# Block-sparse attention and a Hyena mixer in one kernel: mask copies in an earlier slot, stores in a later one, another order before the main loop

## The chip, the cores and the metric

The kernel runs on one core of a Trainium2 chip. The metric is the time of one execution in microseconds (us) on the device. The kernel before takes 345.78 us (median of 3 runs, 345.19 to 347.83).

## The reference

Two parts, one after the other. The first is block-sparse attention: 4 batches x 8 heads, 768 positions, head size 64. Keys are averaged over blocks of 64 positions; each query takes the three blocks with the highest causal gate score, and its own block. The second part, a Hyena mixer, projects the attention's result (768 x 512 for each batch) to three parts, convolves the second with a filter over the sequence by Fourier transforms, multiplies the three and projects once more.

```python
gate_scores = np.einsum('bhsd,bhnd->bhsn', q, k_rep)          # k_rep: block means of k
gate_scores = np.where(causal, gate_scores, -1000000000.0)
top_idx = np.argsort(gate_scores, axis=-1)[..., -top_k:]      # top_k = 3, and the own block
scores = scale * np.matmul(q, k.transpose(0, 1, 3, 2))        # masked to those blocks, causal
attn = softmax(scores);  x = attn @ v
x1, x2, x3 = split(x @ w_proj)
x2_conv = irfft(rfft(x2) * rfft(filter_fft))
out = (x1 * x2_conv * x3) @ w_out
```

## The kernel before

**Slots.** The 32 heads (4 batches x 8) are worked one after the other, each in three slots (`s` = 0, 1, 2). The order of all instructions is written out by hand: the loop at the end of the kernel goes over the slots, and what it emits first stands first on each engine. A slot computes one of three groups of score matmuls (`scores`, L393), their exponential on ACT (L396) and the causal cut of the diagonal blocks on POOL (`diagonals`, L404). One slot later follow the product with the values (`product`, L415), the inverse of the sums on ACT (L422, L423) and, another slot later, the normalisation on DVE (L433).

**Preparing a head.** The sync engine's queue (SP) issues the loads of keys, queries and values some heads ahead (L106, L110, L114), 192 KB each. For head n+4, in slots 0 and 1 of head n: DVE casts the query to fp16 and takes the remainder (`split_query`, L302, L304), POOL casts the key (`cast_key`, L295) and scales the remainder (`low_query`, L307), and SP issues a DMA transpose of both to the tile qkT (`turn_query`, L312). That instruction waits on SP until POOL has written; what stands behind it on SP waits too.

**The mask.** The block choice goes into the scores as 12 additional rows of qkT (rows 64 to 75 of the query's half), which meet one-hot rows on the key's side. For two heads at once, n+2 and n+3 at an even head n: `gate` (slot 1) computes the gate scores on TensorE (L331) and picks the blocks on DVE (L334 to L344); `turn_mask` (slot 2) is a DMA transpose on SP to the tile gmT (L350); `place_mask` copies 12 rows of gmT into each of the two qkT by DMA (L366), in slot 1 of the odd head n+1, behind that slot's `turn_query`. The first scores of an even head need its copy. Heads 0 and 1 have another way, `turn_first_mask`: six transposes on TensorE (L358) and a copy on ACT (L360).

**Units of the mixer.** `plan` puts one unit of the mixer into most slots from head 9 on, for the batch whose attention is done; the last batch's units run after the last head. `unit_out` (L533) computes 128 rows of the result, ACT copies them to the tile osb (L536), and the store (L539) is issued on SP one slot later.

**Setup.** Before the first slot the kernel prepares heads 0 to 3 and the first part of the Fourier tables: products of positions on TensorE, brought into one turn by DVE, POOL and DVE (`phase_round` L199, `phase_turns` L205, `sines` L214 and L215). `small_constants` (POOL) writes the causal bias and own-block tables that `gate` uses. The dictionary `setup` puts further work into slots: the filter's rows are loaded in heads 2 to 4, folded in heads 4 to 6 (`filter_rows`, L588 to L591), and turned into a spectrum in slot 2 of heads 6, 7 and 8 (`filter_spectrum`): after six matmuls each of two or three results is made by one scaled copy on ACT from PSUM (L605) and one combined multiply-add on DVE (L606).

Of the kernel before, what the change touches and what calls it, by code (L numbers as in the profile page):

```python
# [9 lines left out]
FP32 = mybir.dt.float32  # L10
# [7 lines left out]
def kernel(  # L18
# [39 lines left out]
    xtp = ctx.enter_context(tc.tile_pool(name="xtp", bufs=2))  # L58
    p2 = ctx.enter_context(tc.tile_pool(name="p2", bufs=1))
    p2b = ctx.enter_context(tc.tile_pool(name="p2b", bufs=2))  # L60
    outp = ctx.enter_context(tc.tile_pool(name="outp", bufs=3))


    ps_big = ctx.enter_context(tc.tile_pool(name="ps_big", bufs=2, space=bass.MemoryType.PSUM))
# [43 lines left out]
    def load_query(n):  # L108
        queries[n] = hpool.tile([P, SC, D], FP32, name="q_nat", tag="q_nat")
        nc.sync.dma_start(queries[n], q_r[divmod(n, H)])  # L110
# [43 lines left out]
    def key_mask(i):  # L154
        nc.gpsimd.tensor_scalar(qk16s[i][:, 1, :, D:D + NBLK], in0=eblk, scalar1=MASK, scalar2=0.0,
                                op0=ALU.mult, op1=ALU.add)
# [10 lines left out]

    lsc = const.tile([P, 1], FP32)

    def small_constants():  # L170
        nc.gpsimd.memset(cbias, 0.0)
        nc.gpsimd.affine_select(
            out=cbias[0:64], in_=cbias[0:64], compare_op=ALU.is_ge,
            fill=-CBIG, base=0, pattern=[[2, SC], [0, 2], [-1, NBLK]], channel_multiplier=0)
        nc.gpsimd.affine_select(
            out=cbias[64:128], in_=cbias[64:128], compare_op=ALU.is_ge,
            fill=-CBIG, base=1, pattern=[[2, SC], [0, 2], [-1, NBLK]], channel_multiplier=0)
        for h in range(2):
            nc.gpsimd.tensor_scalar(ownm[:, :, h, :], in0=eblk, scalar1=1.0, scalar2=-1.0,
                                    op0=ALU.mult, op1=ALU.add)  # L180

    FC = const.tile([P, HC, F], fp)
    FS = const.tile([P, HC, F], fp)
# [22 lines left out]
                                scalar2=-float(S2), op0=ALU.add, op1=ALU.mult)  # L206


    sign16 = const.tile([P, 1], fp)
    sign = const.tile([P, 1], FP32)  # L210

    def sines(i):
        pr, ka = phases.pop(i)
        nc.vector.tensor_add(pr, pr, ka[:, 0:F])  # L214
        nc.scalar.activation(FS[:, i, :], pr, AF.Sin, bias=0.0, scale=TWO_PI / S2)  # L215
        if i == HC - 1:
            nc.vector.tensor_scalar(sign16, in0=pr[:, 0:1], scalar1=4.0 / S2, scalar2=None,
                                    op0=ALU.mult)
            nc.vector.tensor_copy(sign, sign16)

    def cosines(i):

# [67 lines left out]
                                       in1=kr[:, 0:w, 0, :], op0=ALU.mult, op1=ALU.subtract)  # L290
        sums[g] = kr

    def cast_key(n):
        g, i = group_of[n]
        nc.gpsimd.tensor_copy(qk16s[n % NB][:, 1, :, 0:D], keys[g][:, i])  # L295

    rems = {}

# [230 lines left out]
    def unit_out(st, scn):  # L529
        yT = st["yT"]  # L530
        op = one_tile("op")
        for cc in range(DC):
            nc.tensor.matmul(op, lhsT=yT[:, cc, P * scn:P * (scn + 1)], rhs=wo[:, cc, :],  # L533
                             start=(cc == 0), stop=(cc == DC - 1))
        osb = outp.tile([P, Dm], FP32, name="osb", tag="osb")
        nc.scalar.copy(osb, op)  # L536

        def later():
            nc.sync.dma_start(out[st["b"], P * scn:P * (scn + 1), :], osb)  # L539
        return later  # L540

    X2, X13, F1, F2, O = unit_x2, unit_x13, unit_f1, unit_f2, unit_out

# [49 lines left out]
    def filter_spectrum(j):  # L593
        sl = slice(P * j, P * (j + 1))
        hc, hs_ = pair("hsp", Dm)
        for i in range(HC):
            nc.tensor.matmul(hc, lhsT=FC[:, i, sl], rhs=fil[:, 0, i, :],
                             start=(i == 0), stop=(i == HC - 1))
        for i in range(HC):
            nc.tensor.matmul(hs_, lhsT=FS[:, i, sl], rhs=fil[:, 1, i, :],  # L600
                             start=(i == 0), stop=(i == HC - 1))

        def put(dst, first, s0, second, s1, op):
            t = p2b.tile([P, Dm], FP32, name="turn", tag="t1")
            nc.scalar.mul(t, second, s1)  # L605
            nc.vector.scalar_tensor_tensor(out=dst, in0=first, scalar=s0, in1=t,  # L606
                                           op0=ALU.mult, op1=op)
        cosB = tw0[:, 0:1] if j == 0 else tw[:, 0, j:j + 1]
        put(Asb[:, j, :], hc, tw[:, 0, j:j + 1], hs_, tw[:, 1, j:j + 1], ALU.add)
        put(Bsb[:, j, :], hs_, cosB, hc, tw[:, 1, j:j + 1], ALU.subtract)  # L610
        if j == 0:
            put(A2, hc, tw0[:, 0:1], hs_, tw0[:, 1:2], ALU.add)

    def weights(dst, src, cols, ns):
        nc.gpsimd.dma_start(out=dst[:, ns, cols],
# [4 lines left out]
    def at(n, slot, fn, *args):  # L620
        setup.setdefault((n, slot), []).append((fn, args))

    at(0, 0, key_sums_mm, 2, range(SC))
    at(0, 0, key_sums_copy, 2)
    at(0, 1, key_sums_turn, 2)
    at(0, 1, key_sums_split, 2)
    at(0, 2, gate, [2, 3])
    at(0, 2, turn_mask, [2, 3])
    at(2, 1, turn_weights)
    at(2, 2, make_flip)  # L630
    for i in range(HC):
# [14 lines left out]
    nc.vector.memset(lsc, 1.0)  # L646
    nc.vector.memset(lsc[64:128, :], 1.0 / LO)
    nc.vector.memset(qk16s[0][:, 1, :, D + NBLK:P], 0.0)
    for i in range(HC):
        phase_mm(i)  # L650
    phase_round(0)
# [1 line left out]
    phase_round(1)  # L653
    sines(0)
    phase_turns(1)
    key_mask(0)
    split_query(0)
    cast_key(0)
    low_query(0)
    turn_query(0)  # L660
    key_sums_mm(0, range(SC))
    sines(1)
    key_sums_copy(0)
    key_sums_mm(1, range(SC))
    key_sums_turn(0)
    nc.vector.memset(qk16s[1][:, 1, :, D + NBLK:P], 0.0)
    key_mask(1)
    cast_key(1)
    small_constants()
    split_query(1)  # L670
    low_query(1)
    turn_query(1)
    load_query(3)
    load_key(3)
    load_value(0)
    key_sums_split(0)
    key_sums_copy(1)
    key_sums_turn(1)
    phase_round(2)
    key_sums_split(1)  # L680
    for gm16 in gm16s:
        nc.gpsimd.memset(gm16, 0.0)
    phase_turns(2)
    sines(2)
    id_f16 = const.tile([P, P], fp)
    nc.gpsimd.memset(id_f16, 0.0)
    nc.gpsimd.affine_select(
# [11 lines left out]
    cast_key(2)  # L699
    low_query(2)  # L700
    turn_query(2)
    load_value(1)
    gate([1])
    turn_first_mask(1)
    nc.gpsimd.memset(v16s[0][:, :, D:P], 1.0)
    cast_value(0)
    split_query(3)
    cast_key(3)
    low_query(3)
    turn_query(3)  # L710
    for i in range(1, NB):
        nc.gpsimd.memset(v16s[i][:, :, D:P], 1.0)
    load_key(4)
    load_key(5)
    load_query(4)
    key_loads = {0: [6], 1: [7], 2: [8], 3: [9, 10], 4: [11]}


    xTs, stages, later = {}, {}, []
    for slot in range(max(units) + 1):  # L720
        n, s = divmod(slot, 3)
        todo, later = later, []
        if n < NH:
            if n % H == 0 and s == 0:
                xTs[n // H] = xtp.tile([P, DC, S], fp, name="xT", tag="xT")
            scores(n, s)
            if s == 2:
                scores_left[0] -= 1
        for fn in todo:
            fn()  # L730
        if n < NH:
            diagonals(n, s)
            if s == 0:
                for m in key_loads.get(n, [n + 7]):
                    if m < NH:
                        load_key(m)
                if n + 5 < NH:
                    load_query(n + 5)
                if n + 2 < NH:
                    load_value(n + 2)  # L740
                if n + 2 in group_at and n:
                    key_sums_turn(group_at[n + 2])
                if n + 4 < NH:
                    split_query(n + 4)
                    cast_key(n + 4)
                    low_query(n + 4)
                if n + 2 in group_at and n:
                    key_sums_split(group_at[n + 2])
            elif s == 1:
                if n + 4 < NH:  # L750
                    turn_query(n + 4)
                if n % 2 == 0 and 0 < n < NH - 2:
                    gate([n + 2, n + 3])
                elif n % 2 == 1 and n + 1 < NH:
                    place_mask(n + 1)
                    place_mask(n + 2)
            else:
                if n % 2 == 0 and 0 < n < NH - 2:
                    turn_mask([n + 2, n + 3])
                if n + 1 < NH:  # L760
                    cast_value(n + 1)

            if n + 3 in group_at and n:
                key_sums_mm(group_at[n + 3], (2 * s, 2 * s + 1))
                if s == 2:
                    key_sums_copy(group_at[n + 3])
        for fn, args in setup.get((n, s), []):
            fn(*args)
        for b, fn, *args in units.get(slot, []):
            if b not in stages:  # L770
                stages[b] = new_stage(b, xTs[b])
            act = fn(stages[b], *args)
            if act is not None:
                later.append(act)

        pn, ps = divmod(slot - 1, 3)
        if 0 <= pn < NH:
            product(pn, ps)
            if ps != 1:
                half = min(ps, 1)  # L780
                inverse_sum(pn, half)
                later.insert(0, lambda pn=pn, half=half: normalise(pn, half, xTs[pn // H]))
    for fn in later:
        fn()


# [28 lines left out]
```

## Time and profile before

The profiled execution took 347.45 us; its span, from the first to the last of the program's instructions, is 345.7 us.

| | |
|---|---|
| median of 3 runs | 345.78 us |
| profiled execution, its span | 347.45 us, 345.7 us |
| busy: TensorE (PE) | 268.8 us, 78% |
| busy: weight loads (PEld) | 138.3 us, 40% |
| busy: VectorE (DVE) | 206.4 us, 60% |
| busy: ScalarE (ACT) | 204.4 us, 59% |
| busy: GpSimd (POOL) | 186.1 us, 54% |
| transfers of SP's queue | 43.43 MB, 62.2% of 16 DMA engines |
| transfers of POOL's queue | 2.10 MB, 6.0% |
| mean granted TensorE clock | 0.904 |
| first scores of heads 0, 2, 12, 24 | 18.8, 41.3, 139.6, 242.2 us |

"Busy" is time in which an engine executed. A wait has a releaser, which the profile infers from semaphores: "PE sps L393 <- DMA qkT<-gmT" is idle time of TensorE before the score matmuls that ended when a mask copy landed. SPq is the queue that SP issues DMAs from; its instructions are issues, and the transfers run later on 16 shared DMA engines. POOL's queue casts and loads the weights. The granted clock is the share of full speed that the throttle leaves TensorE.

### The profile page before, as it was taken

To read this page: it belongs to the slowest core of one execution; us is meant where nothing else is said; L and a number is where in the kernel's file an instruction comes from. 1 tells how busy PE (TensorE), PEld (TensorE's weight loads), DVE (VectorE), ACT (ScalarE), POOL (GpSimd) and SP (SyncE) were. 2 spreads that over 40 slices of the span, in tenths; PEclk is the share of its full clock that TensorE was granted. 3 is DMA by queue.
4 is the path that set the end of the run, shared out by engine and by line. 5 is a ranking of instruction groups with operands and counts; after the bars stand their busy time and mean duration, and the time that the engine had idled before them with its cause. 6 is when DMAs were issued, how large, how long until landed. Compare 5 with 4: busy or idle time off the path is not lost.

```text
span 345.7 us, 5124 instructions
## 1 busy us (share of the span) xinstructions
PE 268.8 (78%) x1555; PEld 138.3 (40%) x1555; DVE 206.4 (60%) x568; ACT 204.4 (59%) x326; POOL 186.1 (54%) x336
## 2 busy tenths in 40 slices
PE   4267493967497695889679988995999879989785
PEld 3133241433142252445334544453445446535442
DVE  5616462634456099377945788688357965546750
ACT  2334492755766164557757777676677669953234
POOL 7633261865455229387753375868233847622670
PEclk9996876787769699899969999999699999999999
DMA  8796979998569889768778686667866511021004
GB/s 160 136 192 106 175 168 215 180 189 151 95 105 178 150 121 152 127 108 151 149 163 208 137 194 147 137 100 158 177 151 152 120 53 27 2 93 61 32 0 182
DMA packets 150379, 45.85 MB, mean 133 GB/s; under 512 B 145128, under 2 KB 146512, under 8 KB 150352
## 3 DMA queue, kind: packets, MB, share of 16 engines
q1 hardware_dynamic: 144976, 43.43, 62.2%
q0 software_dynamic: 5376, 2.10, 6.0%
q8 instruction: 12, 0.20, 0.2%
q14 instruction: 15, 0.12, 0.1%
HBM read 24.64 MB, written 6.29 MB: 89 GB/s over the span
## 4 chain that ended last, share of the span: by engine, by line
PE 42%; POOL 14%; ACT 13%; DVE 11%; DMA 10%; issue 7%; SPq 4%; DVEq 0%; ACTq 0%; POOLq 0%
DMA qkT<-gmT 8%; PE sps L393 7%; PE oT L415 6%; PE op L533 5%; ACT ex L396 4%; PE krp L263 4%; SPq L312 3%; ACT den L422 3%; PE x2a L461 3%; PE x2b L461 2%; POOL ex L404 2%; PE x13b L500 2%; PE x13a L500 2%; ACT den L423 2%; POOL PQ L489 1%
## 5 line engine op out<-in xcount | busy, mean ns | idle before, releaser
L396 ACT ACTIVATE ex<-sps 128x1024 f16<-128x1024 f32 (+2 forms) x96 | 88.0, 917 | 59.4 <-PE sps L393 57.4
L404 POOL TENSOR_SCALAR_AFFINE_SELECT ex<-ex 128x128 f16<-128x128 f16 (+1 forms) x128 | 47.3, 380 | 104.2 <-ACT ex L396 103.7
L393 PE MATMUL sps<-qkT 76*128 76x384 f16 (+2 forms) x288 | 62.2, 332 | 33.8 <-DMA qkT<-gmT 33.8
L415 PE MATMUL oT<-ex,v 128*128 128x384 f16 (+2 forms) x288 | 59.7, 314 | 11.6 <-POOL ex L404 6.5
L433 DVE TENSOR_TENSOR xT<-oT,den 64x384 f16<-64x384 f32 x64 | 35.2, 550 | 47.4 <-ACT den L423 45.7
L393 PEld LDWEIGHTS <-qkT 76*128 76x128 f16 x288 | 27.7, 109 | 49.5 <-DMA qkT<-gmT 30.4
L415 PEld LDWEIGHTS <-v 128*128 128x128 f16 x288 | 27.8, 103 | 44.7 <-issue 27.5
L422 ACT ACTIVATE den<-oT 64x384 f32<-64x384 f32 x64 | 31.1, 485 | 22.1 <-PE oT L415 20.9
L500 PEld LDWEIGHTS <-wp 128*128 128x128 f16 x256 | 24.8, 99 | 24.8 <-issue 10.0
L423 ACT ACTIVATE den<-den 64x384 f32<-64x384 f32 x64 | 33.3, 520 | 2.0
L263 PE MATMUL krp<-k_nat,eblk 128*12 128x256 f32 (+2 forms) x132 | 28.3, 356 | 1.9 <-POOL dft_ka L205 1.6
L533 PE MATMUL op<-wo,yT 128*128 128x512 f16 x96 | 27.2, 416 | 2.0 <-POOL yT L525 1.8
L500 PE MATMUL x13b<-xT,wp 128*128 128x384 f16 x116 | 24.1, 331 | 5.9 <-ACT x1sb L504 4.0
L489 POOL TENSOR_TENSOR PQ<-t,t 128x512 f16<-128x512 f32 x12 | 15.2, 1271 | 23.1 <-DVE t L482 22.9
L500 PE MATMUL x13a<-xT,wp 128*128 128x384 f16 x116 | 24.3, 332 | 0.0
L302 DVE CAST qk<-q_nat 128x384 f16<-128x384 f32 x32 | 17.9, 559 | 10.4 <-DMA q_nat<-in_q_dram 10.2
L505 DVE TENSOR_TENSOR gx<-x1sb,x13b 128x384 f32<-128x384 f16 x29 | 16.0, 551 | 12.5 <-PE x13b L500 8.3
L304 DVE TENSOR_TENSOR rem<-q_nat,qk 128x384 f32<-128x384 f32 x32 | 21.2, 664 | 2.5
L536 ACT COPY osb<-op 128x512 f32<-128x512 f32 x24 | 14.0, 585 | 13.6 <-PE op L533 12.6
L307 POOL TENSOR_SCALAR qk<-rem 128x384 f16<-128x384 f32 x32 | 16.3, 510 | 9.3 <-DVE rem L304 6.9
L525 POOL TENSOR_TENSOR yT<-gx,yy 128x384 f16<-128x384 f32 x16 | 16.0, 999 | 6.6 <-DVE yy L521 6.2
L317 POOL CAST v<-v_nat 128x384 f16<-128x384 f32 x32 | 19.0, 593 | 0.0
(129 smaller groups left out, 406.8 us busy)
## 6 DMA issues: line engine op xcount, KB each, us to landing
q_nat<-in_q_dram SPq DMA_DIRECT2D x32, 192.0 KB
k_nat<-in_k_dram SPq DMA_DIRECT2D x32, 192.0 KB
v_nat<-in_v_dram SPq DMA_DIRECT2D x32, 192.0 KB
out_dram<-osb SPq DMA_DIRECT2D x24, 256.0 KB
wp<-in_moe_w_proj_dram POOLq DMA_DIRECT2D x12, 128.0 KB, 5.2
fa<-in_moe_filter_fft_dram SPq DMA_DIRECT2D x3, 256.0 KB
fb<-in_moe_filter_fft_dram SPq DMA_DIRECT2D x3, 256.0 KB
qkT<-gmT SPq DMA_DIRECT2D x30, 18.0 KB
```

Source lines behind the costliest of these rows:

```text
L263: nc.tensor.matmul(sums[g][0:NBLK, 0:w * D], lhsT=eblk[:, c, :], rhs=keys[g][:, 0:w, c, :], start=(c == 0), stop=(c == SC - 1))
L304: nc.vector.tensor_sub(rems[n], q_nat, qk16[:, 0, :, 0:D])
L317: nc.gpsimd.tensor_copy(vals[n][:, :, 0:D], values.pop(n))
L393: nc.tensor.matmul(sps[:, col:col + qe - qs], lhsT=turned[n][0:76, 1, kc, :], rhs=qT[0:76, qs:qe], start=True, stop=True, skip_group_check ...
L396: nc.scalar.activation(ex[:, lo:hi], sps[:, lo:hi], AF.Exp, bias=0.0, scale=scale)
L404: nc.gpsimd.affine_select(out=sub, in_=sub, compare_op=ALU.is_ge, fill=0.0, base=0, pattern=[[0, cnt], [1, P]], channel_multiplier=-1)
L415: nc.tensor.matmul(oT[:, qs - HALF * half:qe - HALF * half], lhsT=vals[n][:, kc, :], rhs=exps[n, src][:, col:col + qe - qs], start=first, ...
L422: nc.scalar.activation(den[64:128, :], oT[64:128, :], AF.Ln, bias=0.0, scale=1.0)
L423: nc.scalar.activation(den[64:128, :], den[64:128, :], AF.Exp, bias=0.0, scale=-1.0)
L433: nc.vector.tensor_tensor(out=dst, in0=oT[0:64, :], in1=den[64:128, :], op=ALU.mult)
L500: nc.tensor.matmul(dst, lhsT=wp[:, dc2, base:base + P], rhs=xT[:, dc2, hs:hs + HALF], start=(dc2 == 0), stop=(dc2 == DC - 1))
L533: nc.tensor.matmul(op, lhsT=yT[:, cc, P * scn:P * (scn + 1)], rhs=wo[:, cc, :], start=(cc == 0), stop=(cc == DC - 1))
```

## The change

- `place_mask` for heads n+1 and n+2 moves from slot 1 of the odd head n, behind `turn_query`, to its slot 0, behind the loads and ahead of the next `turn_query`. It begins with heads 4 and 5: heads 2 and 3 now take the way of heads 0 and 1 (one `gate` each, six transposes on TensorE, a copy on ACT), in slot 2 of head 0 and slot 1 of head 1.
- A store is issued two slots after its unit (one after the last head), from a list, and osb has four buffers in place of three.
- Before the first slot: queries, keys and values of heads 0, 1, 3 and 4 are loaded in another order, some before the transposes of queries 1 and 2; the keys of heads 0 and 1 are cast on ACT in place of POOL; the gate's buffers are cleared on DVE in place of POOL; the last phase step comes earlier; `small_constants` is split in two. The gate and mask of head 1 and the preparation of query 3 move into slot 0 of head 0, query 4 into slot 1.
- `filter_spectrum` copies both results from PSUM on ACT once; the scaled copies are then made by DVE from those copies.
- The sign for the cosine table is computed from the sine table in slot 2 of head 0.

```diff
-    def small_constants():
+    def small_constants(half):
...
+    def time_sign():
+        nc.vector.tensor_scalar(sign, in0=FS[:, 0, 0:1], scalar1=0.0, scalar2=2.0,
+                                op0=ALU.is_gt, op1=ALU.mult)
+        nc.vector.tensor_scalar(sign, in0=sign, scalar1=-1.0, scalar2=None, op0=ALU.add)
...
-        def later():
-            nc.sync.dma_start(out[st["b"], P * scn:P * (scn + 1), :], osb)
-        return later
+        stores.append((slot, out[st["b"], P * scn:P * (scn + 1), :], osb))
...
+        hcs = p2b.tile([P, Dm], FP32, name="hcs", tag="t1")
+        hss = p2b.tile([P, Dm], FP32, name="hss", tag="t2")
+        nc.scalar.copy(hcs, hc)
+        nc.scalar.copy(hss, hs_)
         def put(dst, first, s0, second, s1, op):
-            t = p2b.tile([P, Dm], FP32, name="turn", tag="t1")
-            nc.scalar.mul(t, second, s1)
+            t = p2b.tile([P, Dm], FP32, name="turn", tag="t2")
+            nc.vector.tensor_scalar(t, in0=second, scalar1=s1, scalar2=None, op0=ALU.mult)
             nc.vector.scalar_tensor_tensor(out=dst, in0=first, scalar=s0, in1=t,
                                            op0=ALU.mult, op1=op)
...
     split_query(0)
-    cast_key(0)
+    cast_key(0, nc.scalar.copy)
+    small_constants(0)
     low_query(0)
     turn_query(0)
+    load_query(3)
+    load_key(3)
+    load_value(0)
...
     turn_query(1)
-    load_query(3)
-    load_key(3)
-    load_value(0)
+    load_value(1)
+    load_key(4)
+    load_query(4)
+    phase_round(2)
+    phase_turns(2)
...
     for gm16 in gm16s:
-        nc.gpsimd.memset(gm16, 0.0)
-    phase_turns(2)
-    sines(2)
+        nc.vector.memset(gm16, 0.0)
...
+    def prepare(n, s):
+        if s == 0:
...
+            if n % 2 == 1 and 1 < n < NH - 2:
+                place_mask(n + 1)
+                place_mask(n + 2)
...
+        elif s == 1:
+            if n + 4 < NH:
+                turn_query(n + 4)
+            if n == 1:
+                gate([3])
+                turn_first_mask(3)
+            elif n % 2 == 0 and n < NH - 2:
+                gate([n + 2, n + 3])
...
+    def prepare_first(s):
+        if s == 0:
+            gate([1])
+            turn_first_mask(1)
+            key_sums_mm(2, range(SC))
+            ready_query(3)
+            turn_query(3)
+            load_key(6)
+            load_query(5)
+            load_value(2)
+            for i in range(1, NB):
+                nc.gpsimd.memset(v16s[i][:, :, D:P], 1.0)
+        elif s == 1:
+            key_sums_copy(2)
+            key_sums_turn(2)
+            key_sums_split(2)
+            ready_query(4)
+            turn_query(4)
+        else:
+            gate([2])
+            turn_first_mask(2)
+            cast_value(1)
...
+        while stores and stores[0][0] <= slot - (2 if n < NH else 1):
+            _, dst, osb = stores.pop(0)
+            nc.sync.dma_start(dst, osb)
```

## The prediction

> **What bounds the kernel now.** I read the page's groups first: the score matmuls (L393) are TensorE's largest group, and all of their idle time has one releaser. Columns after the bars: busy us and mean ns, then idle us before and what ended it.
>
> ```profile
> L393 PE MATMUL sps<-qkT 76*128 76x384 f16 (+2 forms) x288 | 62.2, 332 | 33.8 <-DMA qkT<-gmT 33.8
> ```
>
> The table of waits (total us, times, longest) gives the size of one; the chain of waits of the DMA-issuing queue shows what that queue itself stands behind.
>
> ```profile
> PE sps L393 <- DMA qkT<-gmT: 33.8, 10, 6.0
> ```
>
> ```profile
> SPq L539 <- ACT osb L536: 71.0, 24, 17.5
> SPq L312 <- POOL ex L404: 32.9, 10, 6.9
> ```
>
> So TensorE stands still 33.8 us, ten times, always at the first scores of an even head, until that head's mask rows have been copied by DMA. The queue's own timeline says why they come late (start us, issue us):
>
> ```profile
> 47.22 1.24 SPq L350 DMA_TRANSPOSE gmT<-gm  x1
> 48.51 0.58 SPq L581 DMA_DIRECT2D fa<-in_moe_filter_fft_dram  x1
> 49.13 0.43 SPq L582 DMA_DIRECT2D fb<-in_moe_filter_fft_dram  x1
> 49.61 1.02 SPq L106 DMA_DIRECT2D k_nat<-in_k_dram  x2
> 50.67 0.54 SPq L110 DMA_DIRECT2D q_nat<-in_q_dram  x1
> 51.26 1.15 SPq L114 DMA_DIRECT2D v_nat<-in_v_dram  x1
> 52.52 2.89 SPq L312 DMA_TRANSPOSE qkT<-qk  x1
> 55.46 1.52 SPq L366 DMA_DIRECT2D qkT<-gmT  x2
> ```
>
> The masks (L366) go out behind the query transpose (L312), which waits for POOL and needs 2.89 us to issue; the scores of head 4 start at 57.61, after 6.01 us of idling. Last, stretches of the trace: busy time of the engines, granted clock, DMA share, GB/s.
>
> ```profile
> 42.00:44.50 2.50, 2.50 (x21) 1.40 (x20) 0.49 (x2) 2.03 (x3) 1.01 (x3) 0.50 1.11 234
> 44.50:46.50 2.00, 2.00 (x10) 1.18 (x9) 1.89 (x13) 1.92 (x3) 1.01 (x3) 0.50 0.02 2
> 52.00:56.00 4.00, 0.00 (x0) 0.00 (x0) 1.37 (x5) 0.40 (x1) 0.75 (x2) 0.75 1.26 224
> 41.30:139.60 98.30, 69.94 (x355) 33.28 (x356) 52.65 (x155) 56.23 (x85) 52.19 (x95) 0.80 0.93 155
> ```
>
> Heads 2 to 11 (41.3 to 139.6) have no full engine: TensorE 70 of 98 us. The DMA share reads 0.93, but single stretches read 1.26 and others 0.02, so 0.93 is about three quarters of what the engines reach here.
>
> **The masks, heads 4 to 12.** The copies now go out right after the loads of the odd head's first slot, ahead of the query transpose of the second. Two cases. Where transfers are queued up, the copy saves the bytes of the transpose ahead of it: 393 KB at the 234 GB/s above is 1.7 us. That holds at heads 4 (idle 6.01) and 6 (idle 2.93): 2 x 1.7 = 3.4. Where the queue stood waiting for POOL, the copies leave much earlier: head 8, at 83.1 (last load issued) instead of 91.28, so all of its 3.19; head 10, 108.6 instead of 112.48, with 1.7 us of bytes less ahead: landing about 111 where TensorE was free at 110.44, so 4.8 of 5.37; head 12, 130.9 instead of 133.76 and landing near 135, so all 4.6. Together **16.0 us**. What the copies newly wait for on this queue is the landing of the mask transpose itself, issued two to three loads before; at head 4 it was out 5 us before that point.
>
> **The masks, heads 16 to 28.** Idle 2.68, 0.62, 3.23, 0.53. Here something else is late next: at 24 the projection (L533) needs yT, which POOL finishes at 240.63 (start 239.63, 1.00), while it started at 243.01, so 2.4; at 16 POOL ends at 174.19 against 175.94, so 1.7; the small ones whole. **5.2 us.**
>
> **The clock behind the stalls.** TensorE rows right after a stall:
>
> ```profile
> 242.18 1.03 PE L393 MATMUL sps<-qkT 76*128 76x128 f16 x4 [3.23 <-DMA qkT<-gmT]
> 243.01 1.91 PE L533 MATMUL op<-wo,yT 128*128 128x512 f16 x4
> ```
>
> The same groups elsewhere take 0.60 (233.34) and 0.97 (185.08). Over the first five groups after 242.18 (1.03, 1.91, 0.85, 0.95, 1.87) against their undisturbed rows (0.60, 0.97, 0.49, 0.55, 0.97) that is 3.0 us. TensorE is the bound there, so I count 5 us for heads 16 and 24 together, and nothing in heads 2 to 11, where slower matmuls have slack (bounds 0 and 5 x 1.7 = 8 more).
> The Trainium skill (TensorE: Matmul & The Clock Gate, What's actually happening) says that an idle window of about 3.4 us halves the clock until about 3.4 us of work have passed, and speaks against fitting it: "the ramp penalty is <1% of a typical kernel span". By that sentence this term would be under 3.5 us in all; by the rows it is 5.
>
> **Start to head 2.** Removed: the mask memsets from POOL (L682, 2 x 0.74) ahead of the last phase's step, gate and mask of head 1 ahead of the first scores, and the late load of query 4 (issued at 22.61, now behind query 1's transpose at about 11):
>
> ```profile
> 18.76 1.03 PE L393 MATMUL sps<-qkT 76*128 76x128 f16 x4
> 26.64 0.36 DVE L302 CAST qk<-q_nat 128x384 f16<-128x384 f32 x1 [7.70 <-DMA q_nat<-in_q_dram]
> 41.26 1.04 PE L393 MATMUL sps<-qkT 76*128 76x128 f16 x4 [4.63 <-DMA qkT<-gmT]
> ```
>
> Step by step. gps of head 0 comes at 10.2 as before; its DVE chain (0.21+0.22+0.46+0.22+0.22, with gaps 1.5) starts at about 10.6 instead of 13.60, since sines(2) no longer waits for the memsets; six transposes 0.7 and the copy 0.79 put the first scores at 13.8 (before 18.76). Then, in TensorE's order: scores 1.0, gate 1 with its DVE chain 2.3 and transposes 0.7, key sums 2.7: second scores at 20.5 (22.39). Scores 0.9, product 0.8, key-sum turn 0.4: third at 22.6 (29.38, where query 4 was awaited). Scores 0.9, gate 2 with its chain 2.1, transposes 0.7, product 1.1: head 1 at 27.4 (31.25). Its three slots hold 4.3 us of rows as before, plus gate 3 and its transposes 3.0: head 2 at about 35 (41.26). **6.5 us**, from 3 (gates blocking TensorE for 2 us more each) to 9 (query 4 alone costs 7.7 now). The new casts on ACT (by the 0.48 of L504), two memsets on DVE (0.19 for 156 words, so up to 0.5) and the split constants lie under the transfers before 10.2.
>
> **Spectrum.** Before, ACT and DVE hand over three times: ACT is held from 82.85 to 86.60. After, ACT does two copies (0.585, from L536): 1.2 us, so the exponential of head 7, late at 86.50 with its scores out at 83.7, can come 2.6 us earlier. DVE does three multiplies and three combinations, unshown in this form: the multiply lies between the cast at 0.35 (L302, 384 wide; 0.47 for 512) and its stretched rows of 1.15 when POOL is busy (64.94); I take 0.6, nearest to L199's 0.55. 3 x (0.6 + 0.75) = 4.05 from 83.4 ends at 87.4, as now (87.38). **2 us**, from +1 to -4.5.
> The Trainium skill (VectorE: DVE Perf Modes, The perf-mode tier table) gives 1227 ns for 2048 fp32 elements from SBUF; a quarter is 0.31, an estimate, and by it the DVE part ends 0.9 earlier.
>
> **Stores.** The 71.0 us that the queue waits for osb vanish, but TensorE waits for no store; what they delayed are masks, counted above. Nothing (0 to -2).
>
> **Against it.** The query transpose now stands behind two copies (1.5 us) and their wait. In heads 2 to 6 its result is used soon: turn issued by 55.41, gate at 60.25. With head 4 starting 3 to 4 us earlier that slack is gone: 1 us for three pairs, **+3**. Denser loads in the same 98 us: **+2**.
>
> **Sum.** -16.0 - 5.2 - 5 - 6.5 - 2 + 5 = -29.7. The profiled execution took 347.45 (span 345.7 and 1.75 around it), so 317.7; the median shown, 345.78, lies 1.67 lower: **316 us**.
>
> **Rivals.**
> Transfers bound. If a share of 1.0 is all there is, heads 2 to 11 shrink by 7% of 98, 7 us, the start (share 0.92 from 18.8 to 41.3) by 2, and only the late terms 5.2 + 5 stay: -19, 327. For it: 0.93 mean. Against: 1.26 at 52 to 56.
> The clock as well. If warm matmuls also shorten heads 2 to 11 (chain: score and output matmuls 13% of the span) and nothing turns late: -30 - 8 - 3, 305.
> The edit does little: the copies wait for the mask transpose as long as they now wait for the query transpose. The start stays, and a few us: 337 to 345. Against: at head 4 the transpose was out 5 us earlier.
> Slower: the copies' wait holds the queue, so the query transposes behind it land after the gate that reads them, and the gate delays the next masks. Price: 2 us of waiting and 1.5 of issuing in each of 13 pairs, 45 us, against the 34 won: 357. It decides once the hold exceeds the slack of a transpose to its gate; the trace shows 60.25 - 55.41 less about 1 us of landing, 3.8, in the light heads and more in the others, and hardly any wait of that kind today (0.8 us, once).
>
> **How the numbers follow.** Chances: forecast (308 to 322) 0.50; transfers 0.20; clock too 0.15; little 0.08, of which 0.03 within 1%; slower 0.07. About 1% is what a measurement here can tell from no change. The range 302 to 333 takes in the forecast, the transfer case and most of the clock case, and matches the bounds: -45 with every upper end (16 + 5.2 + 13 + 9 + 4.5 + 2 - 5), which is 301; -14 with 3 for the start, 8 for heads 4 to 12, 3 late, 1 for the clock and the spectrum at +1, which is 332. Faster 0.90, same 0.03, slower 0.07.
>
> **What will show it.** The wait of the scores for the mask copy should fall from 33.8 to under 8 us, the rest at heads 4 and 6; first scores near 14, head 2 near 35; the queue's wait for osb gone; granted clock above 0.90 on the mean; ACT's hold at the first spectrum near 1.2 us. It is wrong if a wait of the gate for the query transpose, or of the scores for the copies in their new place, sums to over 15 us.

## The result, and the profile after

The kernel after takes 316.89 us (median of 4 runs, 315.45 to 321.71), the kernel before beside it 346.80 us (345.19 to 348.44): a ratio of 0.912, 95% interval 0.905 to 0.920. The ratio, like all ratios below, compares the fast executions alone and leaves out the slow one of 321.71 us. The forecast was 316 us, the range 302 to 333. The profiled execution took 317.47 us with a span of 315.8 us; the granted TensorE clock rose from 0.904 to 0.951 on the mean.

The line of the score matmuls in the groups (busy us and mean ns, then idle us before and what ended it):

```profile
L393 PE MATMUL sps<-qkT 76*128 76x384 f16 (+2 forms) x288 | 57.4, 311 | 8.4 <-DMA qkT<-gmT 7.6
```

The same matmuls idle 8.4 us instead of 33.8, and they are faster as well: 311 ns on the mean instead of 332. The waits of TensorE in the kernel after (total us, times, longest):

```profile
PE sps L393 <- DMA qkT<-gmT: 7.6, 3, 3.8
...
PE gps L331 <- DMA qkT<-qk: 5.2, 5, 2.7
```

Ten waits for the mask copies have become three, at heads 4, 6 and 12. The gate's wait for a query transpose has grown from 0.8 us (once) to 5.2 us (five times). The waits of SP's queue:

```profile
SPq L790 <- ACT osb L536: 56.2, 13, 17.2
SPq L312 <- POOL ex L404: 31.2, 11, 5.2
...
SPq L366 <- DMA gmT<-gm: 2.0, 3, 0.9
```

The copies themselves (L366) hold the queue for only 2.0 us in their new place. The queue still stands 56.2 us at stores whose osb isn't written yet (71.0 before), but 49.8 of them behind the last head, where only stores are left on it. SP's queue around head 4, the stretch that the prediction showed (start us, us of issuing):

```profile
42.58 1.23 SPq L350 DMA_TRANSPOSE gmT<-gm  x1
43.85 0.58 SPq L578 DMA_DIRECT2D fa<-in_moe_filter_fft_dram  x1
44.48 0.43 SPq L579 DMA_DIRECT2D fb<-in_moe_filter_fft_dram  x1
44.95 1.02 SPq L106 DMA_DIRECT2D k_nat<-in_k_dram  x2
46.02 1.06 SPq L110 DMA_DIRECT2D q_nat<-in_q_dram  x1
47.12 0.90 SPq L114 DMA_DIRECT2D v_nat<-in_v_dram  x1
48.13 1.68 SPq L366 DMA_DIRECT2D qkT<-gmT  x2
49.99 1.46 SPq L312 DMA_TRANSPOSE qkT<-qk  x1
```

The copies now go out between the last load and the query transpose, 5.55 us after the mask transpose (8.24 before). Last, the stretch from 41.30 to 139.60, which held heads 2 to 11 before and holds heads 3 to 13 and the start of 14 now (busy us of PE, PEld, DVE, ACT, POOL, then granted clock, DMA share, GB/s):

```profile
41.30:139.60 98.30, 79.28 (x448) 39.22 (x446) 68.19 (x193) 64.83 (x101) 64.27 (x112) 0.88 0.98 179
```

In the same 98.3 us TensorE does 448 matmuls instead of 355 and the DMA engines move 179 GB/s instead of 155, at a share that only went from 0.93 to 0.98.

Where the 29.9 us of span went, by the starts of the heads' first scores in the two traces:

| | before | after | won | forecast |
|---|---|---|---|---|
| start to head 2 | 41.26 | 37.06 | 4.2 | 6.5 |
| heads 2 to 11 | 98.32 | 80.97 | 17.4 | 13 (16 + 2 - 5) |
| heads 12, 13 | 18.95 | 19.10 | -0.2 | 0 |
| heads 14 to 29 | 132.69 | 124.83 | 7.9 | 10.2 (5.2 + 5) |
| head 30 to the end | 54.48 | 53.84 | 0.6 | 0 |

### The profile page after: what moved, and what is told of

Its sections match the earlier page's. It is cut to its first block, busy times and chain, and to the rows that moved or that the text cites. A ratio compares the mean times of both kernels' runs of the same rounds, so it can differ in the third digit from the quotient of the medians.

```text
span 315.8 us, 5184 instructions
## 1 busy us (share of the span) xinstructions
PE 260.3 (82%) x1567; PEld 136.7 (43%) x1567; DVE 211.8 (67%) x581; ACT 205.2 (65%) x329; POOL 185.5 (59%) x332
## 4 chain that ended last, share of the span: by engine, by line
PE 48%; DVE 13%; ACT 12%; DMA 9%; POOL 8%; issue 6%; SPq 3%; DVEq 0%; ACTq 0%
PE oT L415 7%; DMA qkT<-qk 6%; PE krp L263 6%; PE sps L393 6%; PE op L533 5%; PE x13b L500 4%; ACT ex L396 3%; PE x13a L500 3%; ACT den L422 3%; PE x2a L461 2%; PE x2b L461 2%; ACT den L423 2%; DMA qkT<-gmT 2%; PE rev L585 2%; DVE t L482 1%
## 5 line engine op out<-in xcount | busy, mean ns | idle before, releaser
L415 PE MATMUL oT<-ex,v 128*128 128x384 f16 (+2 forms) x288 | 57.9, 305 | 13.3 <-POOL ex L404 6.2
L393 PE MATMUL sps<-qkT 76*128 76x384 f16 (+2 forms) x288 | 57.4, 311 | 8.4 <-DMA qkT<-gmT 7.6
L433 DVE TENSOR_TENSOR xT<-oT,den 64x384 f16<-64x384 f32 x64 | 35.2, 551 | 37.6 <-ACT den L423 36.3
L393 PEld LDWEIGHTS <-qkT 76*128 76x128 f16 x288 | 26.7, 103 | 23.8 <-DMA qkT<-gmT 8.2
L533 PE MATMUL op<-wo,yT 128*128 128x512 f16 x96 | 24.9, 388 | 1.4 <-POOL yT L525 1.4
L302 DVE CAST qk<-q_nat 128x384 f16<-128x384 f32 x32 | 18.6, 580 | 2.1 <-DMA q_nat<-in_q_dram 2.0
```

What stands on the lines that cost most here:

```text
L393: nc.tensor.matmul(sps[:, col:col + qe - qs], lhsT=turned[n][0:76, 1, kc, :], rhs=qT[0:76, qs:qe], start=True, stop=True, skip_group_check ...
L415: nc.tensor.matmul(oT[:, qs - HALF * half:qe - HALF * half], lhsT=vals[n][:, kc, :], rhs=exps[n, src][:, col:col + qe - qs], start=first, ...
L433: nc.vector.tensor_tensor(out=dst, in0=oT[0:64, :], in1=den[64:128, :], op=ALU.mult)
```

## The experiments

The theory: the copies' place on the queue is what decides, and the start, the spectrum and the stores are small beside it. The rivals: transfers bound these heads in any case; the clock does more than I counted; the copies ahead of the query transposes turn the gate late.

### The copies alone, taken back and put in

First the kernel after with the copies back in slot 1, behind the query transpose:

```diff
-            if n % 2 == 1 and 1 < n < NH - 2:
-                place_mask(n + 1)
-                place_mask(n + 2)
...
                 turn_query(n + 4)
+            if n % 2 == 1 and 1 < n < NH - 2:
+                place_mask(n + 1)
+                place_mask(n + 2)
```

> The changed kernel with one part undone: the mask copies stand again in the odd head's second slot, behind the query transpose. Theory (the place of the copies on the queue is the gain): the waits of the scores for the copies come back at heads 4 to 28, 25 to 30 us in all against 7.6, and the time is 337 to 341 us. Rival (start, stores and spectrum carry most of it): 317 to 325 us, with the wait back but other work late anyway.

Measured: 341.85 us (340.89 to 342.92), ratio to the kernel before 0.985 (0.980 to 0.990). Its wait for the copies:

```profile
PE sps L393 <- DMA qkT<-gmT: 31.9, 10, 5.8
```

With everything else of the change in place, ten waits and 31.9 us are back, and 25 of the 30 us are gone. The other way round, the kernel before with nothing but the copies moved to slot 0, behind the loads (those of heads 2 and 3 too):

```diff
                     load_value(n + 2)
+                if n % 2 == 1 and n + 1 < NH:
+                    place_mask(n + 1)
+                    place_mask(n + 2)
...
                     gate([n + 2, n + 3])
-                elif n % 2 == 1 and n + 1 < NH:
-                    place_mask(n + 1)
-                    place_mask(n + 2)
```

> The kernel before with one part done: the mask copies in the odd head's first slot, behind the loads, also those of heads 2 and 3; nothing else. Theory: wait for the copies under 12 us against 33.8, time 322 to 330 us. Rival (the copies wait for the mask transpose as long as they did for the query transpose, or the query transposes are now late): 338 us or more.

Measured: 323.54 us (322.10 to 324.90), ratio 0.932 (0.925 to 0.938).

```profile
PE sps L393 <- DMA qkT<-gmT: 14.1, 5, 4.1
```

The moved copies alone bring 24 us. That a DMA share of 0.93 meant "full" falls with this run: no byte was taken away, and heads 2 to 11 take 87.8 us instead of 98.3, more than the 7 us that this rival allowed.

### The start alone, the stores, the spectrum

The run with late copies (the first of the two above), and the stores and the spectrum of before as well, so that the start is what is left of the change:

```diff
-    outp = ctx.enter_context(tc.tile_pool(name="outp", bufs=4))
+    outp = ctx.enter_context(tc.tile_pool(name="outp", bufs=3))
...
-        nc.scalar.copy(hcs, hc)
-        nc.scalar.copy(hss, hs_)
+        hcs, hss = hc, hs_
...
-            nc.vector.tensor_scalar(t, in0=second, scalar1=s1, scalar2=None, op0=ALU.mult)
+            nc.scalar.mul(t, second, s1)
...
-        while stores and stores[0][0] <= slot - (2 if n < NH else 1):
+        while stores and stores[0][0] <= slot - 1:
```

> The new order of work up to and in head 0 alone, with the masks of heads 2 and 3 by transposes on TensorE; masks of later heads, stores and spectrum as before. By the two traces the first scores of head 2 come at 37.06 against 41.26, so theory: 4 us less than before, 340 to 343 us. Rival (what is won ahead of the first stall is swallowed there, since the mask of head 4 hangs on the transfers): no change, 345 to 347 us.

Measured: 340.54 us (340.06 to 341.39), ratio 0.981 (0.976 to 0.987); its wait for the copies 27.0 us in nine. Head 2 starts at 37.48 against 41.26, 3.8 us. The 1.9% of this run and the 6.8% of the copies alone make 8.7% together; the whole change has 8.8%. The parts add up, and nothing large is in the rest. While the copies are late, the new spectrum and stores bring nothing: 341.85 us with them, 340.54 without.

The kernel after with stores one slot late:

```diff
-    outp = ctx.enter_context(tc.tile_pool(name="outp", bufs=4))
+    outp = ctx.enter_context(tc.tile_pool(name="outp", bufs=3))
...
-        while stores and stores[0][0] <= slot - (2 if n < NH else 1):
+        while stores and stores[0][0] <= slot - 1:
```

> The changed kernel with its stores again one slot late and osb in three buffers. The prediction gave the stores nothing to -2 us, so undoing them should cost 0 to 2: 317 to 319 us. Rival, read from the run with the masks alone: its heads 16 to 30 take 108.6 us with stores one slot late, the changed kernel's 111.1 with stores two slots late, so the later stores cost about 2.5 us there, and undoing them gives 313.5 to 315 us.

Measured: 315.93 us (315.22 to 318.67), ratio 0.915 (0.910 to 0.920), with the kernel after at 0.912 (0.905 to 0.920). The second slot of delay and the fourth buffer are worth nothing that can be measured.

The kernel after with the spectrum as before:

```diff
-        nc.scalar.copy(hcs, hc)
-        nc.scalar.copy(hss, hs_)
+        hcs, hss = hc, hs_
...
-            nc.vector.tensor_scalar(t, in0=second, scalar1=s1, scalar2=None, op0=ALU.mult)
+            nc.scalar.mul(t, second, s1)
```

> The changed kernel with the spectrum made as before, scaled copies on ACT from PSUM. Prediction: its form was worth 2 us (from -1 lost to 4.5 won), so 317.5 to 321 us with heads 6 to 10 slower by that much. Rival (heads 6 to 10 hang on mask copies and transfers, the spectrum lies beside them): 316 to 317 us.

Measured: 319.41 us (318.02 to 320.40), ratio 0.922 (0.918 to 0.927). Against the store run beside it (0.915) that is 0.7% or 2.6 us, and the two intervals just overlap. The trace puts it in the right place: heads 6 to 9 take 35.2 us here (67.80 to 103.02) and 32.7 in the kernel after (66.21 to 98.94). ACT's and DVE's timelines of the kernel after show why (start us, us, what, idle before and releaser):

```profile
75.02 0.59 ACT L603 COPY hss<-hspb 128x512 f32<-128x512 f32 x1 [0.43 <-PE hspb L597]
76.01 1.02 ACT L396 ACTIVATE ex<-sps 128x1024 f16<-128x1024 f32 x1 [0.40 <-PE sps L393]
```

```profile
75.71 0.61 DVE L607 TENSOR_SCALAR turn<-hss,tw 128x512 f32<-128x512 f32 x1 [2.06 <-ACT hss L603]
76.36 0.75 DVE L608 SCALAR_TENSOR_TENSOR Asb<-hcs,tw,turn 128x512 f16<-128x512 f32 x1
```

The exponential of head 7 starts as soon as its scores are out. In the kernel before it started at 86.50, 2.8 us after its scores, behind the third scaled copy. The multiply and the combination on DVE take 0.61 and 0.75 us here; the forecast had 0.6 and 0.75.

### The clock

The kernel before with matmuls in two of its waits; their products are used by nothing:

```diff
+    WARM = 10
...
+            if s == 0 and n in (16, 24):
+                warm = one_tile("warm")
+                for _ in range(WARM):
+                    nc.tensor.matmul(warm, lhsT=FC[:, 0, 0:P], rhs=wp[:, 0, 0:512], start=True, stop=True)
             scores(n, s)
```

> The kernel before, with 10 additional matmuls of 128x512 on data long there, ahead of the scores of heads 16 and 24, where TensorE waits 2.68 and 3.23 us for the copies; their results are not used. They take about 2.4 us at full clock and end inside the wait. Theory (the slow clock behind a stall costs time of its own, 5 us for these two): 341 to 343 us, and the matmuls after the two waits at full speed. Rival (other engines are late there anyway): 345 to 348 us, with faster matmuls but the same slots.

Measured: 347.15 us (344.83 to 349.26), ratio 1.000 (0.996 to 1.004): nothing. Yet the local effect is there. TensorE's timeline at head 16 in the kernel before, and in this run (its line numbers are one higher) at head 16 and, further on, after the wait at head 20:

```profile
175.94 1.91 PE L533 MATMUL op<-wo,yT 128*128 128x512 f16 x4
```

```profile
176.47 1.03 PE L534 MATMUL op<-wo,yT 128*128 128x512 f16 x4
...
207.60 0.61 PE L394 MATMUL sps<-qkT 76*128 76x128 f16 x4 [1.98 <-DMA qkT<-gmT]
...
210.09 1.91 PE L534 MATMUL op<-wo,yT 128*128 128x512 f16 x4
```

The first output product behind head 16's stall takes 1.03 us instead of 1.91, and heads 16 and 17 take 15.07 us instead of 17.35; heads 24 and 25 15.08 instead of 17.95. But TensorE then reaches heads 20 and 28 early, while the copies come when they came before: those waits grow from 0.62 to 1.98 us and from 0.53 to 2.04, and the slow clock moves there (1.91 at 210.09). 5.2 us were won and given back within the four heads that follow. So this run can't price the clock; a run that fills all waits of 0.5 us and more from head 4 on can:

```diff
+    WARM = {4: 18, 6: 10, 8: 10, 10: 18, 12: 16, 16: 12, 20: 8, 24: 12, 28: 8}
...
+            if s == 0 and n in WARM:
+                warm = one_tile("warm")
+                for _ in range(WARM[n]):
+                    nc.tensor.matmul(warm[:, 0:F], lhsT=FS[:, 0, 0:P], rhs=FS[:, 1, :], start=True, stop=True)
             scores(n, s)
```

> The kernel before with useless matmuls of 128x384 ahead of the scores of heads 4, 6, 8, 10, 12, 16, 20, 24 and 28 (18, 10, 10, 18, 16, 12, 8, 12, 8 of them, 1.3 to 2.9 us at full clock), wherever TensorE waits for mask copies; their results are not used. Theory after the run with two such places (the landing of the next copies sets the pace, so what faster matmuls win is waited away at the next even head): clock near 1 in the mean, 345 to 348 us, waits at heads 20 and 28 grown. Rival (the clock costs 5 us or more by itself): 333 to 341 us.

Measured: 336.32 us (335.18 to 339.58), ratio 0.974 (0.968 to 0.980). After the run before, I had held that the clock costs nothing; that theory fell here. 112 matmuls whose results nobody reads make the kernel 9 us faster. To see where, the same with the heads up to 12 alone:

```diff
-    WARM = {4: 18, 6: 10, 8: 10, 10: 18, 12: 16, 16: 12, 20: 8, 24: 12, 28: 8}
+    WARM = {4: 18, 6: 10, 8: 10, 10: 18, 12: 16}
```

> The kernel before with the same useless matmuls ahead of heads 4, 6, 8, 10 and 12 only; their results are not used. In the run with all nine places, head 16 began 7.9 us earlier than in the kernel before, and the rest won 3.5 us more. Theory (the slow clock costs time in heads 4 to 13, where the prediction had counted nothing for it): head 16 some 8 us earlier and 337 to 340 us. Rival (those heads win nothing by themselves): 343 us or more.

Measured: 338.61 us (337.30 to 340.14), ratio 0.978 (0.970 to 0.985). Head 16 starts at 166.46 instead of 175.12, 8.7 us earlier, and head 30 at 282.65 instead of 291.22, still 8.6 earlier: all of the gain is made in heads 4 to 15 and none of it is given back. 4.7 of it fall in heads 10 and 11 (23.77 to 19.04 us, the wait at head 12 included), where the first units of the mixer run. The trace shows their matmuls at about half the time; that everything behind them on TensorE moves up with them is argued, not tested apart. TensorE there, of the kernel before and then of this run:

```profile
117.28 1.89 PE L461 MATMUL x2a<-wp,xT 128*128 128x512 f16 x4
118.95 1.91 PE L461 MATMUL x2b<-wp,xT 128*128 128x512 f16 x4
```

```profile
114.29 1.04 PE L462 MATMUL x2a<-wp,xT 128*128 128x512 f16 x4
115.17 1.03 PE L462 MATMUL x2b<-wp,xT 128*128 128x512 f16 x4
```

And the two stretches 0 to 140 and 140 to 300, of the kernel before, of the run that fills all nine waits, and of the kernel after:

```profile
0.00:140.00 140.00, 89.92 (x478) 44.56 (x479) 73.66 (x235) 70.56 (x105) 72.84 (x150) 0.83 0.91 155
140.00:300.00 160.00, 141.96 (x888) 75.60 (x887) 110.80 (x294) 114.94 (x187) 94.11 (x166) 0.95 0.63 131
```

```profile
0.00:140.00 140.00, 100.16 (x593) 52.23 (x594) 80.16 (x255) 75.93 (x114) 74.34 (x156) 0.90 0.93 160
140.00:300.00 160.00, 145.33 (x930) 77.99 (x930) 110.83 (x285) 116.19 (x191) 95.55 (x167) 1.00 0.67 131
```

```profile
0.00:140.00 140.00, 104.99 (x619) 54.58 (x620) 92.30 (x286) 85.38 (x130) 85.07 (x169) 0.90 0.92 174
140.00:300.00 160.00, 144.52 (x898) 76.80 (x895) 114.79 (x287) 113.51 (x189) 94.06 (x158) 0.99 0.57 123
```

The kernel after reaches by real work the clock that useless work gives the one before: 0.90 and 0.99, against 0.90 and 1.00. The mean clock by itself doesn't price the time: two executions of the run with stores one slot late had 0.919 and 0.960, and took 316.13 and 315.43 us.

### Where on the queue the copies may stand

The kernel after with the copies ahead of the odd head's loads:

```diff
+            if n % 2 == 1 and 1 < n < NH - 2:
+                place_mask(n + 1)
+                place_mask(n + 2)
             for m in key_loads.get(n, [n + 7]):
...
                 load_value(n + 2)
-            if n % 2 == 1 and 1 < n < NH - 2:
-                place_mask(n + 1)
-                place_mask(n + 2)
```

> The changed kernel with the mask copies at the very head of the odd head's first slot, ahead of the loads. Theory (bytes ahead): two to four loads less, 1.7 to 3.4 us, take away the rest of the wait (7.6 us at heads 4, 6 and 12), 311 to 315 us. Rival (the sync queue now stands until the mask transpose has landed, about 2 us for each pair, with the loads behind it, and these come late for the next head's split): 316 to 321 us, with new waits for q_nat and for qkT.

Measured: 323.54 us (322.37 to 327.00), ratio 0.936 (0.931 to 0.942), 2.1% or 7 us behind the store run beside it. SP's queue first, then the engines:

```profile
SPq L366 <- DMA gmT<-gm: 17.8, 13, 1.8
```

```profile
PE gps L331 <- DMA qkT<-qk: 13.0, 7, 5.9
...
DVE qk L302 <- DMA q_nat<-in_q_dram: 8.8, 5, 3.8
```

The queue now stands at the copies in 13 of the 14 pairs, 1.4 us on the mean, until the mask transpose has landed. The scores hardly wait for the copies any more (0.9 us), but the query loads and transposes behind them are late: the gate waits 13.0 us for the transposes instead of 5.2, and 7.0 us instead of 0.5 for the key sums. In the change itself the loads in between cover the landing, and the hold is 2.0 us.

So the slower rival's waits are real. That the hold by itself makes them isn't shown, for most of the loss is in one place: head 12 takes 15.75 us, against 10.03 in the kernel after. SP's queue ahead of it, then TensorE in it:

```profile
116.96 2.15 SPq L366 DMA_DIRECT2D qkT<-gmT  x2
...
120.95 3.60 SPq L312 DMA_TRANSPOSE qkT<-qk  x1
```

```profile
128.96 0.31 PE L331 MATMUL gps<-kr,qkT 128*128 128x24 f16 x5 [5.88 <-DMA qkT<-qk]
129.11 1.44 PE L474 MATMUL f1a<-x2eo,FC 128*128 128x512 f16 x3
```

This is the one pair that held the queue for only 0.1 us. The transpose behind it needs 3.60 us to issue, where the kernel after has, in the same place:

```profile
116.51 1.46 SPq L312 DMA_TRANSPOSE qkT<-qk  x1
```

It lands late, the gate waits 5.88 us, and the matmuls behind the wait run slowly (1.44 us for three that take 0.81 in the kernel after). From 38 to 140 us the twelve query transposes need 31.8 us to issue in this run and 22.6 in the kernel after. Why they need longer stays open.

In the kernel after, the filter's rows are loaded ahead of the copies for heads 4 and 6. In the next run they stand behind the copies of the odd heads:

```diff
-        at(2 + i, 2, load_rows, i)
+        at(1 + 2 * i, 0, load_rows, i)
```

> The changed kernel with the filter's rows (512 KB a time) loaded in the first slots of heads 1, 3 and 5, behind the mask copies, in place of the third slots of heads 2, 3 and 4. Theory (what is left of the wait at heads 4 and 6, 3.84 and 1.74 us, is bytes queued ahead of the copies): 512 KB less ahead are 2.2 us at 234 GB/s, so 1.6 and 0 are left and the time is 312 to 315 us. Rival (the copies hang on the landing of the mask transpose or on the queue's own issue time): 316 to 318 us with the waits as they are.

Measured: 315.18 us (313.06 to 318.87), ratio 0.908 (0.903 to 0.913): by itself not to be told from the kernel after. With the stores one slot late as well:

```diff
-    outp = ctx.enter_context(tc.tile_pool(name="outp", bufs=4))
+    outp = ctx.enter_context(tc.tile_pool(name="outp", bufs=3))
...
-        at(2 + i, 2, load_rows, i)
+        at(1 + 2 * i, 0, load_rows, i)
...
-        while stores and stores[0][0] <= slot - (2 if n < NH else 1):
+        while stores and stores[0][0] <= slot - 1:
```

> The changed kernel with the filter's rows loaded in the first slots of heads 1, 3 and 5 and the stores one slot late again. If both earlier runs add up: 313 to 315.5 us. If they were scatter: 316 to 318.

Measured: 313.99 us (313.21 to 316.43), ratio 0.909 (0.904 to 0.913), the lowest median of the study, though the intervals overlap with that of the kernel after. The rest of the wait for the copies moves instead of going:

```profile
PE sps L393 <- DMA qkT<-gmT: 7.7, 3, 4.2
```

Head 4 waits 2.36 us instead of 3.84 and head 6 none instead of 1.74, but head 10, now reached as early as the other two allow, waits 4.16 where it waited none. Its copies are issued at 94.74 and TensorE gets them at 99.65, while the DMA share reads 1.37 to 1.39: here the transfers are late. Which of them stand ahead of the copies isn't shown.

Last, that kernel with the query load first in every head's slot, and the copies behind it, but ahead of the loads of key and value:

```diff
+            if n + 5 < NH:
+                load_query(n + 5)
+            if n % 2 == 1 and 1 < n < NH - 2:
+                place_mask(n + 1)
+                place_mask(n + 2)
             for m in key_loads.get(n, [n + 7]):
...
-            if n + 5 < NH:
-                load_query(n + 5)
             if n + 2 < NH:
                 load_value(n + 2)
-            if n % 2 == 1 and 1 < n < NH - 2:
-                place_mask(n + 1)
-                place_mask(n + 2)
```

> The same as the run with rows and stores, and the mask copies behind the query's load but ahead of the key's and the value's. Theory (at the head of the slot the copies held the queue 1.4 us for each pair until the mask transpose had landed, and that made the query transposes late): one load ahead leaves about 0.8 us, so waits of the gate for query transposes of 6 to 9 us instead of 13, waits for the copies under 3 us, time 313 to 317. Rival (any hold in this place costs as much as it saves): 318 to 322.

Measured: 321.62 us (318.61 to 322.67), ratio 0.928 (0.923 to 0.933), 6.8 us behind the run before. Its queue stands 12.4 us at the copies (12 times) and the gate waits 15.2 us for query transposes. Again most of the loss is in head 12 (14.70 us against 8.34), behind a pair that held the queue for 0.1 us and a transpose that needed 4.11 us to issue. With one load ahead the copies still hold the queue 12.4 us; with three it is 2.0 to 3.3. Two were not tried.

## Why the prediction was right

**The main step holds.** The time went where the copies' wait was, and their place on the queue moved it: 25 us taken back by one edit, 24 brought by it alone. That the total of 29.7 us met 29.9 of span is luck: heads 2 to 11 won 4.4 us more than forecast, the start 2.3 less and heads 14 to 29 again 2.3 less.

**The masks, heads 4 to 12.** With 1.7 us saved at heads 4 and 6, 4.3 and 1.2 us should have been left; 3.84 and 1.74 are. At heads 8 and 10, nothing and 0.6 should have been left; nothing is. At head 12 the step "landing near 135, so all 4.6" failed by 1.98 us: I held TensorE's own arrival there fixed. It came 19 us earlier (116.05 against 134.99), while the copies went out at 114.68, only 16 us ahead of the 130.9 that I had put down. They stand behind two table transposes and three loads, which weren't moved.

**The masks, heads 16 to 28, and the clock there.** 5.2 + 5 = 10.2 us were forecast for heads 14 to 29; the profiled execution won 7.9, that of the run with stores one slot late 9.5 (137.37 to 260.55) and that with rows and stores 10.4 (136.17 to 258.49). The sum of the two terms holds; they were not measured apart. What the profiled execution of the kernel after has in addition is one slow spell at head 24 (last section).

**The clock in heads 2 to 11** is the step that failed: "nothing in heads 2 to 11, where slower matmuls have slack". Filling the waits with useless work there wins 8.7 us by head 16, just above the 8 that I had kept as the bound (five waits at 1.7 us, with no row behind the 1.7). TensorE's busy share over that stretch, 70 of 98 us, hid that within it heads 10 and 11 already hold mixer units, whose matmuls behind the wait take 1.89 us instead of 1.04. With the forecast's 13 us net for this stretch, 17.4 came. The kernel after in heads 2 to 11, in the same columns as above:

```profile
37.06:118.03 80.97, 62.47 (x357) 30.61 (x354) 57.10 (x168) 55.06 (x85) 52.80 (x96) 0.87 0.95 172
```

For nearly the same matmuls TensorE is busy 62.47 us instead of 69.94, 7.5 less, at a clock of 0.87 instead of 0.80; its waits for the copies of heads 4 to 12 fell by 14.5 (22.09 to 7.56). So the faster matmuls are measured; how much of the 17.4 is theirs was not separated in the kernel after. The rival "the clock as well" was right in its mechanism; the start, which it kept whole, brought less.

**Start to head 2** was mis-sized: 6.5 forecast, 4.2 measured in the kernel after, 3.8 with the start alone. Up to head 1 the steps hold to half a microsecond: first scores 14.03 (forecast 13.8), second slot 20.26 (20.5), third 22.05 (22.6), head 1 27.04 (27.4). Then the step "Its three slots hold 4.3 us of rows as before, plus gate 3 and its transposes 3.0" gave 7.6 us and measured 10.0. About 1 us of that was misread: in the trace before, the rows of these three slots run from 31.25 to 36.63, 5.4 us. TensorE and DVE there, in the kernel after:

```profile
14.03 1.01 PE L393 MATMUL sps<-qkT 76*128 76x128 f16 x4 [0.88 <-ACT qkT L360]
...
32.92 0.70 PE L358 MATMUL gmp<-id_f,gm 128*12 128x128 f16 x5 [2.57 <-DVE gm L344]
33.41 1.06 PE L263 MATMUL krp<-k_nat,eblk 128*12 128x128 f32 x4
```

```profile
30.81 0.55 DVE L433 TENSOR_TENSOR xT<-oT,den 64x384 f16<-64x384 f32 x1 [3.83 <-ACT den L423]
31.39 0.22 DVE L334 TENSOR_TENSOR ga<-gps,cbias 128x60 f32<-128x60 f32 x1
```

The gate's matmuls are out at 30.20, but its first step on DVE stands behind a normalisation that waits for ACT until 30.78, so it starts at 31.39 and TensorE idles 2.57 us; the key sums behind that wait take 1.06 us for four where the kernel before took 0.61 in this place. I had counted the chain from the matmuls on, without the instruction ahead of it on DVE (0.5 us more than the 3.0), and without the slow matmuls behind it (some 1.2 us).

**Spectrum:** 2 us forecast, 2.6 measured by undoing it. The multiply, for which I had an estimate of 0.31 us from the Trainium skill (VectorE: DVE Perf Modes, The perf-mode tier table), takes 0.49 to 0.65 in its seven executions; the 0.6 taken from the rows was nearer. **Stores:** nothing, and nothing measured; but that the 71.0 us vanish was wrong. 50.6 of them lay behind the last head, where only stores are left, and 49.8 are there still; ahead of that they fell from 20.4 to 6.4. **Against it:** 3 us were counted for gates that wait for query transposes; they wait 4.4 more than before, 2.66 of it at head 8, not in heads 2 to 6 as I placed it. The 2 us for denser loads show no sign: DVE's wait for queries fell from 10.2 to 2.0 us, and without the 7.70 at query 4, which the new start removed, from 2.5 to 2.0.

**The rivals.** Transfers as the bound (327) falls: the stretch from 41.30 to 139.60 moves 15% more at a share of 0.98, and heads 2 to 11 take 81.0 us where this rival allowed no less than 91. That the edit does little falls with the copies alone, which bring 24 us. The slower case is real in the two runs with the copies further ahead, as waits of the gate for late query transposes. That its condition, the hold against the slack of a transpose, decides isn't shown: the largest wait stands behind the one pair that hardly held the queue. Its price was far off: against the 45 us that I summed over 13 pairs (there are 14), the copies at the head of the slot hold the queue 17.8 us and lose 7.

## What to carry to other kernels

In this kernel, a small copy that a busy engine waits for belongs on its queue directly behind the loads that cover its own source's landing: one place too late and it stands behind an instruction that waits for another engine, too early and the queue stands at it, and the query transposes behind it come late. When an engine's waits are summed as a gain, add the work that runs slow behind them in stages where that engine looks only 70% busy, and look at the next wait as well, for time won ahead of a fixed arrival can be given back there, as in the run that filled two waits. Of a step that is moved onto another engine's path, look up what stands ahead of it in that engine's order.

## What was not expected of the hardware

**A slow spell behind short waits, in one run of several.** At head 24 the kernel after idles 0.35, 0.62 and 0.96 us in some 4 us, the run with stores one slot late 0.34, 0.64 and 0.23 in the same place, and the run with the copies ahead of the loads 0.34, 0.50 and 1.21. Their timelines from the last of these waits on, in this order:

```profile
216.88 0.29 PE L331 MATMUL gps<-kr,qkT 128*128 128x24 f16 x5 [0.96 <-DMA qkT<-qk]
217.02 1.73 PE L533 MATMUL op<-wo,yT 128*128 128x512 f16 x4
```

```profile
217.16 0.29 PE L331 MATMUL gps<-kr,qkT 128*128 128x24 f16 x5 [0.23 <-DMA qkT<-qk]
217.30 1.02 PE L533 MATMUL op<-wo,yT 128*128 128x512 f16 x4
```

```profile
225.83 0.29 PE L331 MATMUL gps<-kr,qkT 128*128 128x24 f16 x5 [1.21 <-DMA qkT<-qk]
225.97 1.02 PE L533 MATMUL op<-wo,yT 128*128 128x512 f16 x4
```

In the kernel after some 3.5 us of matmuls at little over half speed follow, and heads 24 and 25 take 18.54 us, against 16.14 in the run with stores one slot late; the granted clock over the two heads is 0.91 and 1.00. But the third run waits longer still, and its matmuls stay fast. So the length of these waits doesn't decide by itself; what does stays open.

**Slow matmuls behind waits cost the kernel before 2.6%** (interval 2.0 to 3.3), measured with work that does nothing. The Trainium skill (TensorE: Matmul & The Clock Gate, What's actually happening) says that for modeling "the ramp penalty is <1% of a typical kernel span". Taken as a bound on all the slow matmuls together, as the prediction took it, that would be under 3.5 us here, an estimate; the run that fills all nine waits shows 9.
